# DeltaNet and FFN on one core: four 64x64 tiles for the recurrence, joins in halves, an earlier inverse, weights on another queue

## The chip, the cores and the metric

The kernel runs on one core of a Trainium2 chip. All data are fp32. The metric is the device time of one execution in microseconds (us). The core has five engines, each with its own instruction stream, which run beside each other and wait for one another by semaphores. The profile names them PE (TensorE matmuls; PEld is its weight loads), DVE (VectorE), ACT (ScalarE), POOL (GpSimd) and SP (SyncE, which here only issues DMAs). "SPq" is SP's queue of DMA issues. An engine runs its instructions strictly in the order in which they were placed, so an instruction that waits holds back all that stand behind it on its engine.

## The reference

Per batch and head (4 x 8, 768 tokens, head size 48), a state matrix is read and updated token by token. The attention output then goes through a layer norm and an FFN of 384 → 1536 → 384 with a residual:

```python
k_n = k / (np.linalg.norm(k, axis=-1, keepdims=True) + 1e-06)
for t in range(S):
    y[:, :, t] = q_t @ state
    v_old = k_t @ state
    state = state + beta_t * outer(k_t, v_t - v_old)
x = y.transpose(0, 2, 1, 3).reshape(4, 768, 384)
xn = (x - mean(x)) / sqrt(var(x) + 1e-06) * g_ln
out = x + relu(xn @ w_ch1) @ w_ch2          # 384x1536, 1536x384
```

(The three lines of the loop are the reference's einsum calls, written as products.) The two weight matrices arrive as 64-bit floats; the kernel reads them as pairs of 32-bit words.

## The kernel before, in words

**Chunks.** The 768 tokens are cut into 12 chunks of 64, and two chunks make a slab. Within a chunk the token loop becomes matrix work: U = X (V − K S) with X the inverse of a triangular 64x64 matrix, Y = Q S + P U (P is the masked product of Q and K), and the state grows by Kᵀ U. One instruction covers 8 heads and a pair of batches: the 128 partitions hold 64 tokens of one batch and 64 of another, and a "group" g is the half of the 16 head rows that are worked together.

**Stages of a slab.** `prep` transposes k and q on PE (`p_t`, L252), evicts them on ACT (`kqt`) and forms the products `p_g` (L263); the K Kᵀ half is evicted by ACT (`gsb`, L268) and stored to DRAM (`gd`, L308), the other half is masked by DVE (`pt`, L271). `blocks` loads the 32x32 diagonal blocks of K Kᵀ of the whole slab from DRAM (`gb`, L338), takes the norms from their diagonal on ACT (`nrm`, L344), and inverts all blocks on DVE in 31 steps of two operations (`tmp` L360, `xb` L365). The result goes to DRAM (`xd`, L369) and back into the layout of the recurrence (`xt`, L372). `join` computes the off-diagonal 32x32 block of the inverse: a DVE transpose (`xn`, L384), 32 matmuls of 32x32 (`p_e`, L391), an ACT eviction (`es`, L395), 32 more (`p_z`, L402), a DVE copy into `xt` (L405).

**Stages of a chunk.** `recur(c, g)` computes K S and Q S against the state (`p_b`, `p_y`, L424), V − K S on DVE (`rhs`, L429), U (`p_u` L438, ACT eviction `u` L440), the state's growth (`p_s` L450, DVE add `s` L457), adds P U to `p_y` (L466), evicts it on ACT (`x_ln`, L471), and prepares the layer norm (L475 to L490, `p_n` and `xnt`). `ffn(c)` has 12 groups of 3 matmuls (`p_h`, L502), each with a relu on ACT (`h_f`, L507), then 2 x 12 matmuls (`p_o`, L513), the residual on DVE (`o`, L520) and the output DMA.

**Weights.** The two matrices come in 24 pieces of 128x384. For each, a DMA brings the word pairs into one of two `words` buffers (`fetch_words`, L147, on SP's queue), and six DVE operations (`to_fp32`, L209, L214, L219, L224, L227, L231) build the fp32 piece `w_sb`. The FFN of the first chunks waits for them.

**What sets the order.** A `Plan` gives every step a due time and writes the program in the order of these times (L549 to L579); a scheduler then fixes each engine's stream from that. The times of a chunk are `T` = 50 apart. For a slab whose first chunk is due at t, the products are due from t−90 to t−55, the inverse from t−55 to t−18 and the join from t−10 to t. The part of the program ahead of the plan (L532 to L547) runs the products and the inverse of slab 0, mixed with the first weight pieces. PSUM has 8 banks: four buffers of tag "att", two banks of tag "two" (`p_g` and `p_s`), two of tag "ffn".

## Time and profile before

| | |
|---|---|
| three runs | 783.5, 784.26, 785.45 us (median 784.26) |
| the profiled execution | 784.72 us, of which the span from first to last instruction is 782.9 us |
| PE busy with matmuls | 622.4 us (79% of the span), 7080 records |
| DVE busy | 337.8 us (43%) |
| ACT busy | 167.5 us (21%) |
| POOL busy | 37.6 us (5%) |
| mean granted TensorE clock | 0.858 |

An fp32 matmul stands as two records in this profile, so the 32 matmuls of one `p_e` read "x64". A row of a timeline gives start, length, engine, line, operation, output and inputs, the tile of the array, the shape, the count, and in brackets the idle time ahead of it with what ended it. A row of stretches gives a stretch from A to B, its length, then the busy time (and the number of records) of each engine, the granted clock as a share of full speed, the share of DMA time and the rate in GB/s.

### The profile page before, as it was taken

What the parts mean: (1) busy time and instruction counts of PE and PEld (TensorE: products, weight loads), DVE (VectorE), ACT (ScalarE), POOL (GpSimd) and SP (SyncE); (2) the same over time, 40 slices, a digit from 0 to 9 for tenths busy, and PEclk for the clock granted to TensorE, in tenths of its full rate; (3) what the DMA queues carried; (4) which work ended last, traced back from release to release, by engine and by line L of the source; (5) the groups of instructions that cost most, each with busy time, mean ns of one, the idle gap of its engine ahead of it and who ended that gap; (6) DMA issues with size and microseconds to landing.
All of it is one profiled execution on the core that took longest, in us unless ns stands there. A gap on an engine that the chain in (4) does not pass through costs nothing.

```text
span 782.9 us, 16117 instructions
## 1 busy us (share of the span) xinstructions
PE 622.4 (79%) x7080; PEld 470.8 (60%) x7080; DVE 337.8 (43%) x822; ACT 167.5 (21%) x380; POOL 37.6 (5%) x56
## 2 busy tenths in 40 slices
PE   4300589969989907999956999965999975999997
PEld 3200577647678606867725877734877745868684
DVE  4597569678331862122772112681211671111100
ACT  4110133211143101422201323201222201212120
POOL 4111001000000110000010000000000000000000
PEclk8555559989899955999985999985999995999999
DMA  9891546441243321044121035122012011000000
GB/s 146 184 159 46 103 110 166 90 82 34 50 99 55 53 58 17 1 89 96 21 67 29 1 77 108 21 43 54 1 39 65 1 43 34 2 11 11 12 10 20
DMA packets 136822, 45.18 MB, mean 58 GB/s; under 512 B 128304, under 2 KB 131376, under 8 KB 136752
## 3 DMA queue, kind: packets, MB, share of 16 engines
q1 hardware_dynamic: 130448, 43.24, 26.9%
q10 hardware_dynamic: 6304, 0.92, 1.0%
q8 instruction: 55, 0.90, 0.5%
q14 instruction: 15, 0.12, 0.1%
HBM read 29.98 MB, written 14.16 MB: 56 GB/s over the span
## 4 chain that ended last, share of the span: by engine, by line
PE 61%; DVE 27%; DMA 6%; issue 3%; ACT 2%; SPq 1%; DVEq 0%; ACTq 0%
PE p_h L502 22%; PE p_o L513 16%; DVE tmp L360 7%; DVE xb L365 7%; DMA words<-in_moe_w_ch_dram 3%; PE p_z L402 3%; PE p_e L391 3%; PE p_g L263 3%; PE p_u L438 3%; PE p_y L466 3%; PE p_t L252 3%; PE p_b L424 2%; PE p_s L450 2%; PE p_y L424 1%; DMA xd<-xb 1%
## 5 line engine op out<-in xcount | busy, mean ns | idle before, releaser
L502 PE MATMUL p_h<-xnt,w_sb 128*128 128x256 f32 x864 | 211.4, 395 | 0.0
L513 PE MATMUL p_o<-w_sb,h_f 128*128 128x384 f32 x576 | 202.4, 496 | 7.1 <-DVE w_sb L231 7.1
L502 PEld LDWEIGHTS p_h<-xnt,w_sb 128*128 128x128 f32 x864 | 162.8, 195 | 26.2 <-ACT ksq L283 0.9
L513 PEld LDWEIGHTS p_o<-w_sb,h_f 128*128 128x128 f32 x576 | 105.3, 191 | 70.8 <-DVE w_sb L231 8.3
L391 PE MATMUL p_e<-xn,gsb 32*32 32x32 f32 x768 | 21.6, 229 | 123.6 <-DVE xn L384 123.6
L391 PEld LDWEIGHTS p_e<-xn,gsb 32*32 32x32 f32 x768 | 20.3, 144 | 127.3 <-issue 70.6
L507 ACT ACTIVATE h_f<-p_h 128x256 f32<-128x256 f32 x144 | 55.2, 383 | 168.7 <-PE p_h L502 168.7
L365 DVE TENSOR_TENSOR xb<-xb,tmp 128x31 f32<-128x31 f32 (+15 forms) x186 | 68.1, 366 | 5.4
L360 DVE TENSOR_TENSOR tmp<-xb,gb 128x31 f32<-128x31 f32 (+15 forms) x186 | 66.4, 357 | 5.5
L457 DVE TENSOR_TENSOR s<-s,p_s 48x384 f32<-48x384 f32 x44 | 24.2, 551 | 100.8 <-PE p_s L450 100.4
L395 ACT ACTIVATE es<-p_e 32x512 f32<-32x512 f32 x24 | 14.1, 589 | 128.5 <-PE p_e L391 128.2
L271 DVE TENSOR_TENSOR pt<-p_g,pmask 128x512 f32<-128x512 f32 x24 | 16.6, 692 | 56.4 <-ACT gsb L268 46.3
L405 DVE COPY xt<-p_z 32x512 f32<-32x512 f32 x24 | 16.4, 684 | 56.0 <-PE p_z L402 55.8
L520 DVE TENSOR_TENSOR o<-p_o,x_ln 128x384 f32<-128x384 f32 x24 | 13.3, 555 | 56.3 <-PE p_o L513 56.2
L475 DVE BATCH_NORM_STATS2 st<-x_ln 128x6 f32<-128x384 f32 x24 | 13.4, 559 | 55.0 <-ACT x_ln L471 54.9
L253 ACT COPY kqt<-p_t 128x512 f32<-128x512 f32 x48 | 28.0, 585 | 38.0 <-PE p_t L252 36.8
L263 PE MATMUL p_g<-kqt 48*64 48x128 f32 (+1 forms) x896 | 30.1, 275 | 6.4 <-ACT gsb L268 3.6
L263 PEld LDWEIGHTS p_g<-kqt 48*64 48x64 f32 x896 | 23.8, 146 | 15.9 <-issue 6.6
L466 PEld LDWEIGHTS p_y<-u,pt 64*64 64x64 f32 x768 | 26.0, 142 | 7.1 <-issue 6.9
L402 PE MATMUL p_z<-xt,es 32*32 32x32 f32 x768 | 25.8, 233 | 5.3 <-ACT es L395 4.5
L466 PE MATMUL p_y<-u,pt 64*64 64x48 f32 x768 | 29.1, 227 | 0.0
L402 PEld LDWEIGHTS p_z<-xt,es 32*32 32x32 f32 x768 | 22.6, 147 | 10.1 <-ACT es L395 7.8
(65 smaller groups left out, 503.3 us busy)
## 6 DMA issues: line engine op xcount, KB each, us to landing
words<-in_moe_w_ch_dram SPq DMA_DIRECT2D x24, 384.0 KB, 3.9
gd<-gsb SPq DMA_DIRECT2D x12, 512.0 KB, 3.2
qpad<-in_q_dram SPq DMA_DIRECT2D x24, 192.0 KB, 4.4
v_raw<-in_v_dram SPq DMA_DIRECT2D x24, 192.0 KB, 4.6
out_dram<-o SPq DMA_DIRECT2D x48, 96.0 KB, 2.2
kpad<-in_k_dram SPq DMA_DIRECT2D x22, 192.0 KB, 4.2
xd<-xb SPq DMA_DIRECT2D x6, 512.0 KB, 2.6
gb<-gd SPq DMA_DIRECT2D x44, 64.0 KB, 3.4
```

The lines of the kernel that those rows point to most:

```text
L252: nc.tensor.transpose(p_t[:, j], src[:, h : h + 2], ident)
L253: nc.scalar.copy(made[c][0][g][:, :, n], p_t)
L263: nc.tensor.matmul(p_g[toks, hp, j, n0:n1], kqt[rows, j, 0, toks], kqt[rows, j, n0:n1, toks])
L360: nc.vector.tensor_tensor(out=t, in0=xb[:, 0:n, j : j + 1].to_broadcast([128, n, w]), in1=gb[:, j : j + 1, j + 1 : BK].to_broadcast([128, ...
L365: nc.vector.tensor_tensor(out=rest, in0=rest, in1=t, op=ALU.subtract)
L391: nc.tensor.matmul(p_e[r1, h], gsb[r0, h, BK:C], xn[r0, h])
L402: nc.tensor.matmul(p_z[r0, h], es[r1, h], xt[r1, h, BK:C])
L457: nc.vector.tensor_tensor(out=new, in0=new, in1=p_s[rows, :, 0 : NP * D].rearrange("p e (j d) -> p e j d", d=D), op=ALU.add,)
L466: nc.tensor.matmul(p_y[toks, h], pt[toks, h], u[toks, h], start=(c == 0 and h == 0), stop=True, skip_group_check=True,)
L502: nc.tensor.matmul(p_h, w1_sb[:, t, f * 128 : (f + 1) * 128], xnt[:, t], start=(t == 0), stop=(t == KC - 1),)
L507: nc.scalar.activation(h_f, p_h, ACTF.Relu)
L513: nc.tensor.matmul(p_o, hs[f][:, g * 128 : (g + 1) * 128], w2_sb[:, f], start=(f == 0), stop=(f == FT - 1),)
```

## The change

1. **K S and Q S on four tiles.** Before, the state was zero-padded to 128 rows so that two heads went through one 128x64 tile: 16 matmuls of N = 96 per chunk and group. Now the state is kept without padding, and 32 matmuls of 48 rows and N = 48 are spread over the four 64x64 tiles in the order (0,0), (1,1), (0,1), (1,0) (`TILES`). Both results share a two-bank PSUM tile `p_by` of a new tag "by" with one buffer. U and P U keep their 16 matmuls each, but go through all four tiles in that order, and so does `p_s`.
2. **Halves put back.** With four tiles the odd heads' halves (the two batches) come out exchanged. `unswap` puts them back when U and Y are evicted: an ACT copy of 128x192, a DVE copy of 64x192 and an ACT copy of 64x192 replace one ACT copy of 128x384.
3. **Joins in halves.** `join` takes a slab's two chunks, and each chunk in two halves of 8 heads. The `p_z` matmuls of one half stand between the `p_e` matmuls of the next, and the evictions are of half the size.
4. **Plan.** `T` is 45. Products are due from t−88 to t−62, the inverse from t−62 to t−26 and the join from t−8 to t. Slab 1 and the first chunks have new times, and the loads of the next slab come later or earlier by new rules.
5. **First loads.** The weight words are fetched from POOL's queue and not SP's. The first q and v loads stand behind the first loads of the inverse, and five weight pieces, not four, stand ahead of it in the program.

PSUM is now two banks "att", two "two" (which `p_u` shares), two "by", two "ffn".

The order of the engines' streams shows what the plan's numbers do. The first place is ACT in the steady part of the program, around the square root `nrm` that opens the inverse of a slab (the fourth of five such in the plan). `h_f` is the relu of one of an FFN's 12 groups, and `xnt` the layer norm's last step ahead of that FFN. Before:

```order
L268 COPY gsb<-p_g 128x2x4x64
L490 COPY xnt<-p_n 128x3x128
L283 ACTIVATE ksq<-kpad_77 128x384 x2
L507 ACTIVATE h_f<-p_h 128x256
L286 ACTIVATE knrm<-ksum 128x16
L507 ACTIVATE h_f<-p_h 128x256 x2
L440 COPY u<-p_u 128x384
L507 ACTIVATE h_f<-p_h 128x256 x4
L471 COPY x_ln<-p_y 128x384
L479 ACTIVATE rstd<-mv,eps 128x1
L507 ACTIVATE h_f<-p_h 128x256 x2
L344 ACTIVATE nrm<-gb 128x32
```

And with the change:

```order
L265 COPY gsb<-p_g 128x2x4x64
L430 COPY u<-p_u 128x4x48
L432 COPY u<-p_u 64x4x48
L430 COPY x_ln<-p_by 128x4x48
L432 COPY x_ln<-p_by 64x4x48
L503 ACTIVATE rstd<-mv,eps 128x1
L514 COPY xnt<-p_n 128x3x128
L531 ACTIVATE h_f<-p_h 128x256 x2
L341 ACTIVATE nrm<-gb 128x32
```

Nine relus stood between the last eviction of the products (`gsb`) and `nrm`; now there are two, with the evictions of U and Y of a group ahead of them.

The second place is PE at the join of a slab. `p_o` is the second half of the FFN that stands ahead of it. Before:

```order
L466 MATMUL p_y<-u,pt 64x48 x16
L513 MATMUL p_o<-w_sb,h_f 128x384 x10
L391 MATMUL p_e<-xn,gsb 32x32 x32
L402 MATMUL p_z<-xt_133,es 32x32 x32
L391 MATMUL p_e<-xn,gsb 32x32 x32
L489 MATMUL p_n<-ident,xn_ln 128x128 x3
L402 MATMUL p_z<-xt_134,es 32x32
L424 MATMUL p_b<-s_141,kqt 64x96 x5
L402 MATMUL p_z<-xt_134,es 32x32 x31
L502 MATMUL p_h<-xnt,w_sb 128x256 x3
```

And with the change:

```order
L537 MATMUL p_o<-w_sb,h_f 128x384 x10
L448 MATMUL p_by<-s_131,kqt 64x48 x32
L392 MATMUL p_e<-xn,gsb 32x32 x32
L412 MATMUL p_z<-xt_123,es 32x32 x16
L464 MATMUL p_u<-rhs,xt_123 64x48 x16
L490 MATMUL p_by<-u,pt 64x48 x16
L392 MATMUL p_e<-xn,gsb 32x32 x2
L412 MATMUL p_z<-xt_123,es 32x32 x2
```

The next chunk's `p_by` now stands ahead of the join, and U and P U of its first group stand between the join's halves.

The third place is DVE at the start, where the inverse of slab 0 begins (`tmp`, `xb`) and the weight pieces are decoded (`part`, `power`, `man`, `full`, `w_sb`). Before, six pieces stood ahead of `gb<-gb,db`, which opens the inverse, and two were woven into it:

```order
L352 TENSOR_TENSOR gb<-gb,db 128x1024
L209 TENSOR_SCALAR part<-words 128x384
L360 TENSOR_TENSOR tmp<-xb,gb 128x31
L214 TENSOR_SCALAR power<-part 128x384
L365 TENSOR_TENSOR xb<-xb,tmp 128x31
L219 TENSOR_SCALAR man<-words 128x384
L360 TENSOR_TENSOR tmp<-xb,gb 128x60
L224 SCALAR_TENSOR_TENSOR full<-words,man 128x384
```

With the change nine stand ahead of it, ten are woven into it in the same manner (one operation of a piece, one of the inverse), and three more follow before the first `xn`:

```order
L349 TENSOR_TENSOR gb<-gb,db 128x1024
L216 TENSOR_SCALAR man<-words 128x384
L357 TENSOR_TENSOR tmp<-xb,gb 128x31
L268 TENSOR_TENSOR pt<-p_g,pmask 128x2x4x64
L362 TENSOR_TENSOR xb<-xb,tmp 128x31
L221 SCALAR_TENSOR_TENSOR full<-words,man 128x384
L357 TENSOR_TENSOR tmp<-xb,gb 128x60
L224 SCALAR_TENSOR_TENSOR full<-words,full 128x384
```

So 22 of the 24 pieces stand ahead of the first `xn` on DVE, where there were 10.

The diff, cut to what matters:

```diff
     def ps_att(shape, name):
-        return psum.tile(shape, FP32, name=name, tag="att", bufs=4)
+        return psum.tile(shape, FP32, name=name, tag="att", bufs=2)
 
     def ps_two(shape, name):
         return psum.tile(shape, FP32, name=name, tag="two", bufs=1)
+
+    def ps_by(shape, name):
+        return psum.tile(shape, FP32, name=name, tag="by", bufs=1)
 
...
             words.append(early_pool.tile([128, WN, 2], U32, name="words", bufs=2))
-            nc.sync.dma_start(
+            nc.gpsimd.dma_start(
                 out=words[-1].rearrange("p n w -> p (n w)"), in_=pieces[len(words) - 1][1]
...
-    for c in range(2):
-        load(qpads[c], q, c, (nc.sync,))
-    for c in range(2):
-        vs[c] = loads.tile([128, GH, D], FP32, name="v_raw")
-        load(vs[c], v, c, (nc.sync,))
...
-    states = [const.tile([128, 2, NP, 2, D], FP32, name=f"s{g}") for g in range(2)]
+    states = [const.tile([128, 2, NP, D], FP32, name=f"s{g}") for g in range(2)]
...
+    N_JOIN = 2
+    def join(chunks):
+        last = None
+        for c in chunks:
+            xt, gsb = xts[c % NXT], grams.pop(c)[0]
+            xn = work.tile([128, GH, BK], FP32, name="xn", bufs=1)
+            nc.vector.transpose(xn, xt[:, :, 0:BK])
+            for g in range(2):
+                heads = range(g * H, (g + 1) * H)
+                p_e = ps_att([128, H, BK], "p_e")
+                for h in heads:
+                    for e in range(2):
+                        r0 = slice(e * C, e * C + BK)
+                        r1 = slice(e * C + BK, (e + 1) * C)
+                        nc.tensor.matmul(p_e[r1, h % H], gsb[r0, h, BK:C], xn[r0, h])
+                    if last:
+                        last_z(*last, h % H)
+                if last:
+                    end_z(*last)
+                es = work.tile([128, H, BK], FP32, name="es", bufs=2)
+                for e in range(2):
+                    r1 = slice(e * C + BK, (e + 1) * C)
+                    nc.scalar.mul(es[r1], p_e[r1], -1.0)
+                last = (xt, g, es, ps_att([128, H, BK], "p_z"))
+                yield
+        for h in range(H):
+            last_z(*last, h)
+        end_z(*last)
+        yield
+    def last_z(xt, g, es, p_z, h):
         for e in range(2):
             r0 = slice(e * C, e * C + BK)
+            r1 = slice(e * C + BK, (e + 1) * C)
+            nc.tensor.matmul(p_z[r0, h], es[r1, h], xt[r1, g * H + h, BK:C])
+    def end_z(xt, g, es, p_z):
+        for e in range(2):
+            r0 = slice(e * C, e * C + BK)
+            nc.vector.tensor_copy(out=xt[r0, g * H : (g + 1) * H, BK:C], in_=p_z[r0])
...
+    TILES = ((0, 0), (1, 1), (0, 1), (1, 0))
+    def half(e):
+        return slice(C * e, C * e + C)
+    def unswap(dst, src):
+        nc.scalar.copy(dst[:, :, 0], src[:, 0])
+        nc.vector.tensor_copy(out=dst[half(0), :, 1], in_=src[half(1), 1])
+        nc.scalar.copy(dst[half(1), :, 1], src[half(0), 1])
 
...
+        p_by = ps_by([128, 2, 512], "p_by")[:, :, 0 : 2 * NP * D].rearrange(
+            "p n (m j d) -> p n m j d", m=2, d=D
+        )
         if c:
-            p_b = ps_att([128, H, D], "p_b")
-            for n, dst in ((0, p_b), (1, p_y)):
+            for n in range(2):
                 for j in range(NP):
-                    for e in range(2):
-                        toks = slice(C * e, C * e + C)
+                    for hp, e in TILES:
+                        rows = slice(DP * hp, DP * hp + D)
                         nc.tensor.matmul(
-                            dst[toks, 2 * j : 2 * j + 2], kqt[:, j, n, toks], s[:, e, j],
-                            start=(j == 0), stop=(n == 0), skip_group_check=True,
+                            p_by[half(e ^ (hp & n)), hp, n, j], kqt[rows, j, n, half(e)], s[rows, e, j],
+                            start=(n == 0 and j == 0), stop=(n == 0), skip_group_check=True,
                         )
...
+        p_u = ps_two([128, 2, 512], "p_u")[:, :, 0 : NP * D].rearrange("p n (j d) -> p n j d", d=D)
+        for j in range(NP):
+            for hp, e in TILES:
+                nc.tensor.matmul(
+                    p_u[half(e ^ hp), hp, j], xt[half(e), 2 * j + hp], rhs[half(e), 2 * j + hp]
+                )
         u = work.tile([128, H, D], FP32, name="u")
+        unswap(u.rearrange("p (j n) d -> p j n d", n=2), p_u)
         yield
         if c < NCH - 1:
             p_s = ps_two([128, 2, 512], "p_s")
+            for j in range(NP):
+                for hp, e in TILES:
+                    nc.tensor.matmul(
+                        p_s[DP * hp : DP * hp + D, e, j * D : (j + 1) * D],
+                        kp[half(e), 2 * j + hp, 0:D], u[half(e), 2 * j + hp],
+                    )
             for hp in range(2):
+                new = s[DP * hp : DP * hp + D]
                 nc.vector.tensor_tensor(
                     out=new, in0=new,
+                    in1=p_s[DP * hp : DP * hp + D, :, 0 : NP * D].rearrange("p e (j d) -> p e j d", d=D),
+                    op=ALU.add,
                 )
             yield
+        for j in range(NP):
+            for hp, e in TILES:
                 nc.tensor.matmul(
+                    p_by[half(e ^ hp), hp, 1, j], pt[half(e), 2 * j + hp], u[half(e), 2 * j + hp],
+                    start=(c == 0 and j == 0), stop=True, skip_group_check=True,
                 )
         y = xs[c][:, g]
+        unswap(y.rearrange("p (j n d) -> p j n d", n=2, d=D), p_by[:, :, 1])
         yield
...
-        first.spread(prep_g(c), 4, 0, 4)
-    first.spread(weights(0, 4), 4, 2, 6)
+        first.spread(prep_g(c), 4, 4 * c, 4 * c + 4)
+    first.spread(weights(0, 5), 5, 0, 8)
     first.run()
-    for _ in blocks(0, (nc.sync, nc.scalar)):
+    inverse = blocks(0, (nc.sync, nc.scalar))
+    next(inverse)
+    for c in range(2):
+        load(qpads[c], q, c, (nc.sync,))
+    for c in range(2):
+        vs[c] = loads.tile([128, GH, D], FP32, name="v_raw")
+        load(vs[c], v, c, (nc.sync,))
+    for _ in inverse:
         pass
     first = Plan()
     for c in range(2):
         first.spread(prep_p(c), 5, 0.1 * c, 4)
-    first.spread(weights(4, 6), 2, 2, 4)
+    first.spread(weights(5, 6), 1, 3, 4)
     first.run()
     for c in (2, 3):
         load_all(c)
-    for _ in join(0):
-        pass
-
-    T = 50
-    starts = [0, 16, 90] + [120 + T * i for i in range(NCH - 2)]
-    ends = [12, 36, 120] + starts[4:]
+
+    T = 45
+    starts = [0, 16, 84] + [114 + T * i for i in range(NCH - 2)]
+    ends = [12, 36, 114] + starts[4:]
     plan = Plan()
-    plan.spread(join(1), N_JOIN, 2, 8)
+    plan.spread(join(range(2)), 5, -1, 0)
     plan.spread(weights(6, NW // 2), NW // 2 - 6, 0, 20)
     plan.spread(weights(NW // 2, NW), NW - NW // 2, 20, 52)
     for c in range(NCH):
         t0, t1 = starts[c], ends[c]
         plan.once(t0, begin, c)
-        if c < 2:
-            for g in range(2):
-                plan.spread(recur(c, g), N_RECUR, t0 + g, t1)
-        else:
-            plan.spread(in_turn(recur(c, 0), recur(c, 1)), 2 * N_RECUR, t0, t1)
+        plan.spread(in_turn(recur(c, 0), recur(c, 1)), 2 * N_RECUR, t0, t1)
     ffn_0 = ffn(0)
     plan.spread(ffn_0, FT, 12, 32, whole=False)
-    plan.spread(ffn_0, FT, 48, 66)
-    plan.spread(ffn(1), N_FFN, 66, 120)
+    plan.spread(ffn_0, FT, 48, 64)
+    plan.spread(ffn(1), N_FFN, 64, 114)
     for c in range(2, NCH):
         plan.spread(ffn(c), N_FFN, starts[c + 1], starts[c + 1] + T)
     for m in range(1, NSL):
         chunks = range(SLAB * m, SLAB * m + SLAB)
         t = starts[SLAB * m]
-        times = (t - 90, t - 55, t - 18, t - 10) if m > 1 else (12, 33, 74, 82)
+        times = (t - 88, t - 62, t - 26, t - 8) if m > 1 else (4, 22, 62, 76)
         if m > 1:
             for c in chunks:
-                plan.once(t - 99, load_all, c)
+                plan.once(t - 89 - 40 * (c % SLAB == 0 and m > 2), load_all, c)
         plan.spread(in_turn(*(prep(c) for c in chunks)), SLAB * N_PREP, times[0], times[1])
         plan.spread(blocks(m, (nc.sync,)), N_BLOCKS + 1, times[1], times[2])
-        plan.spread(in_turn(*(join(c) for c in chunks)), SLAB * N_JOIN, times[3], t)
+        plan.spread(join(chunks), 5, times[3], t)
     plan.run()
```

54 lines of the change are left out of this document (4 added, 50 removed).

## The prediction

> **What bounds the kernel now.** I read the chain that ended last first, then the waits, then the span cut at the starts of the joins.
>
> ```profile
> PE 61%; DVE 27%; DMA 6%; issue 3%; ACT 2%; SPq 1%; DVEq 0%; ACTq 0%
> ```
>
> ```profile
> PE p_e L391 <- DVE xn L384: 123.6, 10, 56.5
> ```
>
> The chain runs over PE, but 27% of it is DVE, and PE's longest waits stand at one place: the join waits for `xn`, the end of the inverse. I cut the span there (stretch, length, then busy us and records of PE, PEld, DVE, ACT, POOL, clock, DMA share, GB/s):
>
> ```profile
> 0.00:84.87 84.87, 15.10 (x288) 12.52 (x289) 58.43 (x146) 14.17 (x27) 17.28 (x31) 0.61 0.78 139
> 84.87:201.10 116.23, 103.57 (x1114) 79.95 (x1114) 80.68 (x195) 27.66 (x64) 5.23 (x6) 0.85 0.41 91
> 201.10:294.77 93.67, 69.89 (x1061) 53.60 (x1060) 46.44 (x112) 22.11 (x49) 5.06 (x6) 0.87 0.32 62
> 294.77:414.90 120.13, 103.43 (x1180) 77.63 (x1181) 46.32 (x113) 27.51 (x63) 4.82 (x6) 0.88 0.24 50
> 414.90:534.45 119.55, 103.11 (x1181) 77.31 (x1182) 46.31 (x113) 27.51 (x63) 4.81 (x6) 0.89 0.24 50
> 534.45:651.03 116.58, 103.07 (x1180) 77.27 (x1181) 42.90 (x109) 25.31 (x57) 0.36 (x1) 0.90 0.13 31
> 651.03:782.90 131.87, 124.18 (x1079) 92.50 (x1079) 16.76 (x35) 23.24 (x57) 0.00 (x0) 0.94 0.05 11
> ```
>
> A steady slab takes 120 us, of which PE is busy 103. For the slab from 414.90, the same view of PE and of DVE alone (the last two rows are the inverse's lines L360 and L365):
>
> ```profile
> 428.25:496.82 68.57, 68.57 (x719) 0.98 0.25 53
> 496.82:521.31 24.49, 24.48 (x196) 1.00 0.23 42
> 521.31:534.45 13.14, 0.00 (x1) 0.58 0.36 85
> ```
>
> ```profile
> 496.82:527.60 30.78, 28.27 (x78) 0.93 0.21 40
> 496.82:527.60 30.78, 10.51 (x31) 0.93 0.21 40
> 496.82:527.60 30.78, 11.75 (x31) 0.93 0.21 40
> ```
>
> And the events of the inverse, from the timelines of ACT, SP, DVE and PE, with the median from issue to landing of the load `gb`:
>
> ```profile
> 475.40 0.59 ACT L268 COPY gsb<-p_g 128x512 f32<-128x512 f32 x1 [1.77 <-PE p_g L263]
> ```
>
> ```profile
> 478.96 1.89 SPq L338 DMA_DIRECT2D gb<-gd  x4
> 527.60 0.34 SPq L369 DMA_DIRECT2D xd<-xb  x1
> ```
>
> ```profile
> gb<-gd SPq DMA_DIRECT2D x44, 64.0 KB, 3.4
> ```
>
> ```profile
> 253.88 0.25 ACT L344 ACTIVATE nrm<-gb 128x32 f32<-128x32 f32 x1
> ...
> 496.82 0.25 ACT L344 ACTIVATE nrm<-gb 128x32 f32<-128x32 f32 x1
> ```
>
> The products are done at 476.0, and the block load lands at about 480.85 + 3.4 = 484.2. But `nrm` runs at 496.8, since it stands on ACT behind nine relus, which come as fast as PE's `p_h`: 12.6 us late by order alone. From there it is 30.8 us to the store of the inverse (527.60) and 6.85 us through DRAM and the transpose to the first `p_e` (534.45). PE runs out of work at 521.3 and stands 13.1 us. So a slab is 81.9 (join to `nrm`) + 30.8 + 6.85 = 119.55 us, and whoever moves `nrm` forward shortens it, until PE's own work (about 106) is the limit.
>
> **The change part by part.** The PE rows used:
>
> ```profile
> 201.11 1.20 PE L391 MATMUL p_e<-xn,gsb 32*32 32x32 f32 x64
> ...
> 414.90 1.92 PE L391 MATMUL p_e<-xn,gsb 32*32 32x32 f32 x64 [13.41 <-DVE xn L384]
> ...
> 428.25 2.93 PE L502 MATMUL p_h<-xnt,w_sb 128*128 128x256 f32 x6
> ...
> 435.13 1.13 PE L438 MATMUL p_u<-rhs,xt 64*64 64x48 f32 x32
> 436.19 2.86 PE L502 MATMUL p_h<-xnt,w_sb 128*128 128x256 f32 x12
> 438.98 0.79 PE L450 MATMUL p_s<-u,kpad 64*48 64x48 f32 x32
> ...
> 455.86 0.88 PE L424 MATMUL p_b<-s,kqt 128*64 128x96 f32 x16
> ...
> 457.33 2.85 PE L513 MATMUL p_o<-w_sb,h_f 128*128 128x384 f32 x8
> ...
> 492.58 1.14 PE L466 MATMUL p_y<-u,pt 64*64 64x48 f32 x32
> 493.64 5.45 PE L502 MATMUL p_h<-xnt,w_sb 128*128 128x256 f32 x24
> ```
>
> *Tiles.* K S with Q S take 455.86 to 457.33 = 1.47 us per group; U takes 435.13 to 436.19 = 1.06, and P U 492.58 to 493.64 = 1.06. The growth takes 0.79. That is 4.4. The records of U and P U, over two diagonal tiles, cost 33 ns each; those of the growth, which already alternates over more tiles, 24.7; those of the 32x32 `p_e` at full clock 1.20/64 = 18.8. The price of 64x48 records over four tiles is not in the trace. Its bounds are 18.8 ns (overlap as in `p_e`) and 33 (none). I take 18.8 to 20, since the rows fall with the number of tiles: 64 x 19 = 1.2 for K S and Q S, 0.6 each for the other three, 3.0 in all. Gain 1.3 us per group, 5 per slab; at 24.7 it is 0.4, and at 33 about −0.9.
>
> The Trainium skill, "TensorEngine Tiling (Array Packing)", section Instruction Overhead, speaks against this part: about 60 cycles go to each matmul, and one should not take tiles out of a dimension that is already small. With its figure of 60 cycles, I estimate 25 ns a record at 2.4 GHz and 1.6 us for K S and Q S, no gain there. The 18.8 ns of `p_e` don't agree with it.
>
> *Halves put back.* Each eviction of U and Y becomes three smaller ones over ACT and DVE. For their price I take the `nrm` row (0.25, nearly no data) as the floor and `gsb` (0.59, more data) as the ceiling. Off the chain of the slab they cost nothing: ACT is busy 27.5 of 120 us. On DVE, 8 of some 0.3 us per slab are 2.4 us, about half inside the inverse. The wait of the growth and of P U for U grows by a few tenths; PE has FFN matmuls between. Without that cover it would be 24 x 0.5 = 12 us. Two PSUM waits are new: `p_by` has one buffer, so a group's K S waits for the eviction of the last group's Y, and `p_u` shares two banks with `p_s` and `p_g`, so it waits for their evictions (0.6 as `gsb`). In the new order FFN matmuls of 1.4 us or more stand between, which hides them; inside the join they don't, and what waits behind them there is the rest of the join. They are among its 1.5 us of waits below.
>
> *Join.* 414.90 to 428.25 = 13.35 us now, at a clock that has fallen (`p_e` 1.92 against 1.20) and with waits for each eviction in turn. In halves, with U and P U of one group and most of a `p_by` between, I reckon 256 records at 19 to 30 ns (4.9 to 7.7), 2.2 of other work and about 1.5 of waits: about 10, bounds 9 and 13.
>
> *Plan.* In the new order of the streams, between the join and `nrm` PE has the same work as in 428.25:496.82, less seven groups of `p_h` (two relus for nine). One group is (438.98 − 436.19)/2 = 1.4, so 9.8. U, growth and P U of the second chunk's group also stand behind it now (2.9), what moved into the join is gone (2.6), and the tiles save 3: 68.57 − 18.3 = 50. So `nrm` comes 10 + 50 = 60 us after the join's start. The load will not hold it: the last `gsb` stands some 18 us of PE work ahead, and its way to the landed load was 8.2. The inverse: 22.3 busy us in its two lines, and 3.4 for the operations that open it, with 6.8 of other DVE work woven in now that PE is not idle beside it: 32.5. Then 6.85. Sum 99.4. PE's limit: 10 for the join, and 93.06 (68.57 + 24.49) less 5.2 for tiles and 2.2 moved, 85.7, and 1.5 where `rhs` and `xn` stand between `p_by` and `p_e`: 97.2. The later of the two decides: 99.5 for the slabs of 120, 98.5 for that of 116.6, which has less DVE work. Nothing else is late next: PE's wait of 13 goes to about 2. The slab from 201.10 has its `nrm` at 253.88, 52.8 after the join; the new order has seven relus ahead of it for twelve (−7), and −2.7 of tiles and join: 84.
>
> *First loads.* On DVE the start looks thus:
>
> ```profile
> 43.08 1.23 DVE L352 TENSOR_TENSOR gb<-gb,db 128x1024 f32<-128x1024 f32 x1 [0.60 <-DVE db L349]
> 44.22 0.35 DVE L209 TENSOR_SCALAR part<-words 128x384 uint32<-128x384 uint32 x1
> ...
> 47.35 0.35 DVE L209 TENSOR_SCALAR part<-words 128x384 uint32<-128x384 uint32 x1
> ...
> 74.28 0.21 DVE L365 TENSOR_TENSOR xb<-xb,tmp 128x31 f32<-128x31 f32 x1
> ```
>
> ```profile
> words<-in_moe_w_ch_dram SPq DMA_DIRECT2D x24, 384.0 KB, 3.9
> ```
>
> A woven piece costs about 1.8 us (47.35 − 44.22, less 1.3 of inverse in between). Ten instead of two make the inverse of slab 0 some 14 longer, with fewer other operations in it: its end moves from 74.5 to 86, and the first join, 10 us behind it, to 97. This needs words to land in time. The trace has no fetch on POOL's queue. If one takes L to land, two buffers give a piece every (L + 2.8)/2 us, with 2.8 the six operations. L = 3.9, as on SP, costs nothing; 6 gives 93 for the end of the inverse, 8 gives 106. POOL's fetches wait for a buffer, and behind them on POOL stand the scaling of v and the diagonal copy for the inverse; both come later than the fetch needs its buffer. I take 97, bounds 95 and 115. In return the weights are there when the FFN starts (DVE is free of 12 pieces in that slab), so the second stretch keeps PE's 103.6 less 4 for tiles and 4 for join and clock: 95.5.
>
> The Trainium skill, "SBUF — State Buffer", section "SBUF: two separate sides", warns of this very queue: descriptors of a DMA issued from GpSimd are written by GpSimd's cores, which are locked out while DVE runs some operations, so the DMA waits for DVE. No run here shows such a fetch yet.
>
> *The tail* has no inverse: 131.9 − 5 (tiles) − 3.4 (join) − 1 (clock) = 122.5.
>
> **Sum.** 97 + 95.5 + 84 + 99.5 + 99.5 + 98.5 + 122.5 = 696.5, and 1.8 around the span (784.72 − 782.9): 698 us, where the profiled execution has 784.72 and the median of the runs is 784.26.
>
> **The rivals.**
> - *Records don't overlap* (0.15). At 25 to 33 ns a record the tiles give nothing, PE's limit per slab is 105 and decides: five slabs 5.5 longer and the tail 5, 730. For it: 33 ns for U now. Against it: 18.8 for `p_e`.
> - *Words come late* (0.14). L of 6 to 8 us puts the first join at 104 to 116; the rest is as forecast: 705 to 717, say 716.
> - *The change doesn't move the inverse* (0.06). `nrm` still waits, for a load that is late on SP behind v, k and q. Then only tiles (5 per slab) and joins (3) remain, cut to some 20 in all by the chain that still ends in DVE: 765. Against it: the load has 10 us to spare.
> - *Slower* (0.05). POOL's fetches starve DVE: 22 of 24 pieces stand ahead of the first `xn` in DVE's stream, so DVE, and with it the inverse, goes at the rate of the fetches. The gain of 86 is lost when the first join comes at 183, that is with 22 pieces in some 173 us, 7.9 each, L = 13 us. From there on the kernel is slower: at L = 15, 807.
>
> **How the numbers follow.** The forecast has 0.60. The range of 678 to 732 takes in the second rival and the first to its end; below, it has L at 3.9 with slabs at PE's bound and a join of 9. Left out are the third and fourth and some of the rest. Runs lie within 0.3% of each other, which is what a measurement can tell from no change: faster by more 0.93, the same 0.02, slower 0.05.
>
> **What would show it.** `nrm` some 60 us after a steady join's start, not 82; PE's wait for `xn` at the joins near 2 us, not 13; `p_by` of 64 records in about 1.2 us; U and P U in 0.6. The first `p_e` near 97, and DVE's waits for `words` near nothing. It is wrong if steady slabs stay above 106, if records of 64x48 keep 25 ns or more, or if the first join comes after 115.

## The result

The change makes the kernel faster: 722.55 us (median of four runs, 720.92 to 724.42) against 784.35 before, a ratio of 0.921 with an interval of 0.9185 to 0.924. The profiled execution has a span of 719.1 us. The forecast was 698, and 678 to 732 its range: the direction and most of the size were right, and 24 us of the expected gain are missing.

The span of the changed kernel, cut at the starts of its joins as before (stretch, length, busy us and records of PE, PEld, DVE, ACT, POOL, clock, DMA share, GB/s):

```profile
0.00:107.97 107.97, 17.02 (x289) 13.73 (x289) 86.94 (x219) 14.27 (x27) 37.92 (x55) 1.00 0.79 153
107.97:201.87 93.90, 89.58 (x1254) 69.41 (x1255) 54.41 (x134) 30.43 (x77) 4.73 (x6) 1.00 0.28 62
201.87:290.28 88.41, 70.84 (x1176) 50.10 (x1176) 49.52 (x125) 23.38 (x60) 5.83 (x6) 0.91 0.32 67
290.28:394.33 104.05, 98.87 (x1309) 72.63 (x1309) 49.18 (x125) 29.52 (x75) 5.04 (x6) 0.91 0.29 56
394.33:497.03 102.70, 97.02 (x1309) 71.04 (x1309) 49.23 (x125) 29.50 (x75) 5.04 (x7) 0.93 0.28 57
497.03:596.08 99.05, 95.86 (x1245) 70.01 (x1245) 45.71 (x119) 27.21 (x69) 1.31 (x2) 0.93 0.15 36
596.08:719.10 123.02, 116.77 (x1208) 86.31 (x1207) 20.69 (x48) 25.11 (x69) 0.00 (x0) 0.95 0.06 14
```

| stretch | before | forecast | measured | missed by |
|---|---|---|---|---|
| to the first join | 84.9 | 97 | 108.0 | +11.0 |
| first join to second | 116.2 | 95.5 | 93.9 | −1.6 |
| second to third | 93.7 | 84 | 88.4 | +4.4 |
| third to fourth | 120.1 | 99.5 | 104.05 | +4.6 |
| fourth to fifth | 119.6 | 99.5 | 102.7 | +3.2 |
| fifth to sixth | 116.6 | 98.5 | 99.05 | +0.6 |
| tail | 131.9 | 122.5 | 123.0 | +0.5 |

So the miss lies in two places: the start (11 of 22.6) and the three stretches from the second join to the fifth (12.2 together).

The clock column of the first two stretches can't be relied on. It reads 1.00 there, though `p_e` of the first join takes 1.92 us, as it does at 290.28, where the column reads 0.50, and not 1.20 as at 394.33:

```profile
107.97 1.92 PE L392 MATMUL p_e<-xn,gsb 32*32 32x32 f32 x64 [56.29 <-DVE xn L384]
```

**A steady slab.** The events of the slab from 394.33, as the timelines of ACT, SP and PE have them:

```profile
437.40 0.58 ACT L265 COPY gsb<-p_g 128x512 f32<-128x512 f32 x1 [1.77 <-PE p_g L260]
...
457.33 0.25 ACT L341 ACTIVATE nrm<-gb 128x32 f32<-128x32 f32 x1
```

```profile
440.99 1.89 SPq L335 DMA_DIRECT2D gb<-gd  x4
```

```profile
489.29 0.53 SPq L366 DMA_DIRECT2D xd<-xb  x1
```

```profile
394.33 1.20 PE L392 MATMUL p_e<-xn,gsb 32*32 32x32 f32 x64 [1.94 <-DVE xn L384]
...
397.09 1.55 PE L464 MATMUL p_u<-rhs,xt 64*64 64x48 f32 x32 [0.52 <-DVE xt L417]
...
404.98 0.90 PE L513 MATMUL p_n<-ident,xn_ln 128*128 128x128 f32 x3
...
407.60 5.75 PE L526 MATMUL p_h<-xnt,w_sb 128*128 128x256 f32 x18
...
439.40 0.68 PE L464 MATMUL p_u<-rhs,xt 64*64 64x48 f32 x32
...
442.14 0.57 PE L475 MATMUL p_s<-u,kpad 64*48 64x48 f32 x32
...
445.43 0.68 PE L490 MATMUL p_by<-u,pt 64*64 64x48 f32 x32
...
454.31 1.15 PE L448 MATMUL p_by<-s,kqt 48*64 48x48 f32 x64
...
497.03 1.20 PE L392 MATMUL p_e<-xn,gsb 32*32 32x32 f32 x64 [2.26 <-DVE xn L384]
```

`nrm` now stands 63.0 us behind the join (82 before), the inverse takes 32.0, the way through DRAM to `p_e` 7.7; PE waits 2.3 at the join, not 13. What came forward is the products: the last `gsb` starts 43.1 us behind the join, where it was 60.5. `nrm` is still late by the order on ACT, for `gb` is issued by 442.9 and lands 2.7 to 3.3 us after its issue, some 11 us ahead of `nrm` (12.6 before). The seven relus that no longer stand ahead of `nrm` are PE work that now comes later, but other PE work stands between `gsb` and `nrm` in their place. The records of the recurrence are as fast as hoped: 1.15/64 = 18 ns for K S and Q S, 0.68 us for U and for P U. But the join is longer than forecast. From the first `p_e` to the first `p_h` it takes 13.3 us, and U at 397.09 needs 1.55 us where U at 439.40 needs 0.68. The clock goes with it (same columns as above):

```profile
392.39:394.33 1.94, 0.00 (x2) 0.01 (x1) 1.88 (x4) 0.43 (x2) 0.66 (x2) 1.00 0.78 122
394.33:397.09 2.76, 1.89 (x96) 1.67 (x96) 0.44 (x2) 1.50 (x4) 1.07 (x1) 1.00 0.42 92
397.09:400.83 3.74, 2.92 (x64) 2.35 (x65) 1.38 (x3) 0.63 (x2) 0.00 (x0) 0.52 0.02 4
400.83:403.58 2.75, 2.59 (x117) 2.37 (x117) 1.82 (x5) 1.38 (x4) 0.00 (x0) 0.50 0.00 0
403.58:407.60 4.02, 4.02 (x107) 3.38 (x103) 1.59 (x5) 1.52 (x4) 0.00 (x0) 0.50 0.02 6
407.60:410.00 2.40, 2.40 (x10) 1.95 (x7) 0.83 (x2) 0.00 (x0) 0.00 (x0) 0.50 0.02 7
```

From 397.1 to 410 the granted clock is 0.50. PE waits 1.9 us ahead of the join and some 0.9 between its first steps, and after that it runs at half speed for 13 us, though it is busy most of the time. At the join at 596.08, where PE does not wait for `xn`, the clock falls too (0.51 from 602 to 604), after gaps of 0.7, 0.5 and 0.4 us.

**The start.** DVE's and ACT's rows around the first inverse:

```profile
36.08 0.26 ACT L341 ACTIVATE nrm<-gb 128x32 f32<-128x32 f32 x1 [3.54 <-DMA gb<-gd]
```

```profile
37.38 0.36 DVE L206 TENSOR_SCALAR part<-words 128x384 uint32<-128x384 uint32 x1 [1.15 <-DMA words<-in_moe_w_ch_dram]
...
41.56 0.36 DVE L206 TENSOR_SCALAR part<-words 128x384 uint32<-128x384 uint32 x1 [1.16 <-DMA words<-in_moe_w_ch_dram]
...
48.03 0.17 DVE L342 TENSOR_SCALAR nrm<-nrm 128x32 f32<-128x32 f32 x1
...
50.32 2.34 DVE L349 TENSOR_TENSOR gb<-gb,db 128x1024 f32<-128x1024 f32 x1
...
96.56 0.20 DVE L362 TENSOR_TENSOR xb<-xb,tmp 128x31 f32<-128x31 f32 x1
...
107.20 0.70 DVE L384 STREAM_TRANSPOSE xn<-xt 128x512 f32<-128x512 f32 x1
```

```profile
35.87 0.54 POOL L150 DMA_DIRECT2D words<-in_moe_w_ch_dram  x1 [4.57 <-DVE full L224]
```

`nrm` is ready at 36.3, and DVE takes it up at 48.0: the weight pieces stand ahead of it in DVE's order, and they wait for their words. A piece comes every 4.2 us (37.38, 41.56). The words fetched at 35.87 are used at 41.56 as soon as they land, so landing takes some 5.7 us here, while 3.9 is the median of all 24 fetches. The inverse opens at 50.3 (43.1 before) and ends at 96.8, not 86. The first `xn` stands behind three more pieces, which cost it little: its load `xt` is issued from 99.9 to 101.9 and lands up to 5.0 us later.

### The profile page after: what moved, and what is told of

It is laid out like the page before. It is cut to its first block, busy times and chain, and to the rows that moved or that the text cites. A ratio compares the mean times of both kernels' runs of the same rounds, so it can differ in the third digit from the quotient of the medians.

```text
span 719.1 us, 17676 instructions
## 1 busy us (share of the span) xinstructions
PE 586.0 (81%) x7784; PEld 433.2 (60%) x7784; DVE 355.7 (49%) x894; ACT 179.4 (25%) x452; POOL 59.9 (8%) x80
## 4 chain that ended last, share of the span: by engine, by line
PE 54%; DVE 30%; DMA 7%; issue 3%; ACT 3%; SPq 2%; POOL 0%; DVEq 0%; ACTq 0%; POOLq 0%
PE p_h L526 19%; PE p_o L537 17%; DVE tmp L357 9%; DVE xb L362 8%; PE p_t L249 3%; PE p_g L260 3%; PE p_by L448 2%; DMA words<-in_moe_w_ch_dram 2%; PE p_z L412 2%; PE p_u L464 2%; PE p_e L392 2%; PE p_by L490 2%; SPq L116 1%; PE p_n L513 1%; PE p_s L475 1%
## 5 line engine op out<-in xcount | busy, mean ns | idle before, releaser
L362 DVE TENSOR_TENSOR xb<-xb,tmp 128x31 f32<-128x31 f32 (+15 forms) x186 | 64.2, 345 | 4.5
L392 PEld LDWEIGHTS p_e<-xn,gsb 32*32 32x32 f32 x768 | 18.5, 132 | 76.6 <-DVE xn L384 73.0
L448 PEld LDWEIGHTS p_by<-s,kqt 48*64 48x64 f32 x1408 | 26.7, 143 | 13.1 <-issue 9.8
L453 DVE TENSOR_TENSOR rhs<-v_raw,p_by 128x384 f32<-128x384 f32 x22 | 12.1, 552 | 43.7 <-PE p_by L448 40.8
L400 ACT ACTIVATE es<-p_e 32x256 f32<-32x256 f32 x48 | 18.0, 375 | 61.4 <-PE p_e L392 55.7
L448 PE MATMUL p_by<-s,kqt 48*64 48x48 f32 x1408 | 31.5, 231 | 2.0 <-ACT x_ln L432 2.0
L250 ACT COPY kqt<-p_t 128x512 f32<-128x512 f32 x48 | 27.9, 585 | 19.2 <-PE p_t L249 12.6
L417 DVE COPY xt<-p_z 32x256 f32<-32x256 f32 x48 | 20.0, 417 | 25.3 <-PE p_z L412 24.8
L280 ACT ACTIVATE ksq<-kpad 128x384 f32<-128x384 f32 x24 | 12.5, 521 | 67.9 <-DVE ksum L281 51.1
L351 POOL COPY xb<-db 128x32 f32<-128x32 f32 x6 | 3.5, 584 | 273.9 <-DVE db L346 273.9
```

Source lines behind the costliest of these rows:

```text
L250: nc.scalar.copy(made[c][0][g][:, :, n], p_t)
L362: nc.vector.tensor_tensor(out=rest, in0=rest, in1=t, op=ALU.subtract)
L392: nc.tensor.matmul(p_e[r1, h % H], gsb[r0, h, BK:C], xn[r0, h])
L417: nc.vector.tensor_copy(out=xt[r0, g * H : (g + 1) * H, BK:C], in_=p_z[r0])
L448: nc.tensor.matmul(p_by[half(e ^ (hp & n)), hp, n, j], kqt[rows, j, n, half(e)], s[rows, e, j], start=(n == 0 and j == 0), stop=(n == 0), ...
```

## The experiments

The scheduler writes all streams anew for each kernel, so an edit of one part also moves a few instructions elsewhere. Each kernel was timed in three rounds beside the kernel before.

**Words on SP's queue again.**

```diff
-            nc.gpsimd.dma_start(
+            nc.sync.dma_start(
                 out=words[-1].rearrange("p n w -> p (n w)"), in_=pieces[len(words) - 1][1]
```

> The changed kernel with the weight words fetched from SP's queue again, all else as changed. In its order seven weight pieces stand ahead of the inverse of slab 0 and one is woven into it (the changed kernel: nine and ten), and 15 stand behind the first xn (2). Theory A (the late first join of 108.0 us comes from the pieces that DVE decodes ahead of and inside the inverse, not from the chip's start): first p_e at 76 to 82 us, and the weights come later, so the stretch to the second join grows from 93.9 to 105 or more; sum of both 183 to 195 against 201.9; whole kernel 705 to 716. Rival B (the start is bound by something else, such as the products or the block load): first p_e stays above 100, kernel within 3 us of 722. Rival C (late weights hold the FFN): second join after 202, kernel 723 to 740.

Measured: 712.38 us (707.87 to 714.7). The first stretches of this kernel, and the first wait of the FFN for weights in its PE timeline:

```profile
0.00:75.23 75.23, 16.54 (x288) 13.25 (x288) 54.20 (x132) 13.10 (x24) 14.46 (x29) 0.79 0.78 128
75.23:195.73 120.50, 95.87 (x1225) 68.41 (x1225) 84.78 (x220) 30.28 (x77) 7.42 (x8) 0.76 0.46 107
```

```profile
147.74 2.93 PE L537 MATMUL p_o<-w_sb,h_f 128*128 128x384 f32 x4 [7.32 <-DVE w_sb L228]
```

The first join comes at 75.2, 33 us earlier, and the second at 195.7 against 201.9. Of the 33 us, 27 are given back, since DVE decodes the pieces later (busy 84.8 in the second stretch, against 54.4) and the FFN waits for them. Both joins lie just outside what Theory A expected, the first 0.8 us early and the second 0.7 late; the kernel's time is inside, and outside the ranges of both rivals. Fetching the words on POOL's queue costs 10 us. Six of them show in these two stretches, and there it is DVE's order that does it: nine pieces ahead of the inverse and ten in it, for seven and one.

**The recurrence as before** (wide matmuls against the padded state, one eviction), in the changed plan:

```diff
-    states = [const.tile([128, 2, NP, D], FP32, name=f"s{g}") for g in range(2)]
+    states = [const.tile([128, 2, NP, 2, D], FP32, name=f"s{g}") for g in range(2)]
...
+                            dst[toks, 2 * j : 2 * j + 2], kqt[:, j, n, toks], s[:, e, j],
...
-        unswap(u.rearrange("p (j n) d -> p j n d", n=2), p_u)
+        nc.scalar.copy(u, p_u)
...
-        return psum.tile(shape, FP32, name=name, tag="att", bufs=2)
+        return psum.tile(shape, FP32, name=name, tag="att", bufs=4)
...
-            pt = work.tile([128, H, C], FP32, name="pt", bufs=7)
+            pt = work.tile([128, H, C], FP32, name="pt", bufs=6)
```

> The changed kernel (plan, halved joins, first loads) with the recurrence as before: K S and Q S of 128 rows and N = 96 against the zero-padded state, U and P U over two tiles, one ACT copy per eviction, four att buffers, and six pt buffers for seven (for space). Theory A (tiles save 4.3 - 2.8 = 1.5 us of PE per group and chunk, and PE's order carries nrm and so the slab): 22 groups x 1.5 = 33 slower at most, 745 to 758 us. Rival (the tiles lie off the path, since the slab ends with the inverse, and the three-part evictions cost as much as they save): 715 to 732.

Measured: 732.86 us (731.83 to 734.32), 10 more than the changed kernel. Its fourth and seventh stretch:

```profile
397.20:499.55 102.35, 100.24 (x1181) 74.58 (x1181) 46.88 (x117) 28.19 (x67) 4.86 (x6) 0.97 0.29 56
...
600.81:730.00 129.19, 123.00 (x1084) 90.45 (x1083) 17.83 (x40) 23.84 (x61) 0.00 (x0) 0.97 0.06 14
```

The steady slab is as long with the old tiles (102.35) as with the new (102.70). Of the other two steady slabs one is 0.7 us shorter and one 2.2 longer. Most of the 10 us come from the tail (129.2 against 123.0) and the stretch after the first join (99.1 against 93.9). In the steady slabs PE is busy 100.2 us for 97.0: the new tiles free 1.5 us per group, but a part of that comes back as PE time at the lower clock (0.93 for 0.97), and the rest as idle time. Neither theory's interval was hit exactly; the rival's reason holds for the steady slabs, Theory A's for the two ends.

**The plan's numbers of before**, with tiles, halved joins and first loads as changed:

```diff
-    T = 45
-    starts = [0, 16, 84] + [114 + T * i for i in range(NCH - 2)]
+    T = 50
+    starts = [0, 16, 90] + [120 + T * i for i in range(NCH - 2)]
...
-        times = (t - 88, t - 62, t - 26, t - 8) if m > 1 else (4, 22, 62, 76)
+        times = (t - 90, t - 55, t - 18, t - 10) if m > 1 else (12, 33, 74, 82)
...
-                plan.once(t - 89 - 40 * (c % SLAB == 0 and m > 2), load_all, c)
+                plan.once(t - 99, load_all, c)
```

> The changed kernel with the plan's numbers of before (T = 50, products t-90 to t-55, inverse t-55 to t-18, join t-10 to t, loads at t-99, slab 1's old times); tiles, halved joins and first loads as changed. Theory A (the plan moved nrm from 82 to 63 us behind a join): nrm at 74 to 80 and steady slabs of 112 to 117 us for 103; kernel 755 to 775. Rival (the gain came from tiles and joins alone): steady slabs at 103 to 106, kernel 720 to 735.

**The plan's numbers of the change alone**, in the kernel before (the same lines the other way round):

> The kernel before with the plan's numbers of the change alone (T = 45, products t-88 to t-62, inverse t-62 to t-26, join t-8 to t, slab 1's and the loads' new times); tiles, joins, first loads as before. Theory A (the plan is what moved the steady slabs from 120 to 103, and the tiles lie off the path there): steady slabs 101 to 106, first join at 85, kernel 715 to 735. Rival (without the shorter tiles PE's work is the bound again, or the whole joins cost more in this place): steady slabs 107 to 112, kernel 740 to 760.

Measured: 782.22 us (777.15 to 786.54) without the new plan, 726.9 us (724.61 to 729.07) with it alone. One steady slab of each, the old plan first:

```profile
432.86:546.51 113.65, 97.12 (x1309) 72.37 (x1309) 49.48 (x125) 29.49 (x75) 4.80 (x6) 0.88 0.25 53
```

```profile
383.05:488.49 105.44, 102.07 (x1182) 76.27 (x1181) 46.43 (x113) 27.47 (x63) 4.66 (x6) 0.95 0.28 55
```

The plan alone brings 57 of the change's 62 us (784.35 to 726.9 and to 722.55). Beside it the other parts nearly cancel: the tiles with their evictions are worth 10, the words on POOL's queue cost 10. Without it tiles, halves and first loads together bring next to nothing: they shorten the steady slab from 119.6 to 113.65, and the start, 25 us later at the first join than in the kernel before (110.2 for 84.9), eats it. Two of its three steady slabs are as expected, the third 1.2 us shorter; the kernel was slower than expected because the second and third stretch grew as well, to 110.0 and 98.7 from the 93.9 and 88.4 of the changed kernel.

**Whole joins**, that is the function `join` of the kernel before, in the changed kernel:

```diff
-    N_JOIN = 2
+    N_JOIN = 3
...
-    def join(chunks):
+    def join(c):
```

> The changed kernel with the join of before (a chunk's 32 p_e, one eviction es, 32 p_z, one copy), tiles, plan and first loads as changed. Theory A (a join's length is set by its chain of waits and by the clock, granted at 0.50 in it): halves save a little, 1 to 3 us per join, kernel 728 to 740. Rival (halves bring nothing, since the half clock sets the length): 719 to 726. Rival 2 (the finer halves cost more than they hide): below 719.

Measured: 723.6 us (722.01 to 727.71), not to be told from 722.55. The halves bring nothing that can be measured.

**One copy per eviction**:

```diff
-        nc.scalar.copy(dst[:, :, 0], src[:, 0])
-        nc.vector.tensor_copy(out=dst[half(0), :, 1], in_=src[half(1), 1])
-        nc.scalar.copy(dst[half(1), :, 1], src[half(0), 1])
+        nc.scalar.copy(dst.rearrange("p j n d -> p n j d"), src)
```

> The changed kernel with one ACT copy of 128x384 per eviction of U and Y, as before; the odd heads' halves stay exchanged, so the numbers belong to the wrong batch and this part of the work is left out. Theory A (the three-part eviction costs a few tenths in the join alone): 716 to 722 us. Rival (it eats what the tiles save, by DVE time inside the inverse and by the wait for U): 705 to 713.

Measured: 718.08 us (717.18 to 720.63), a ratio to the kernel before of 0.9145 (0.911 to 0.918) against 0.921. Putting the halves back costs some 4 us. They don't lie in the steady slabs (105.1, 104.3 and 99.4). The second and third stretch are shorter (91.9 and 83.5 us for 93.9 and 88.4), but the kernel with whole joins, which puts the halves back too, also has 84.0 in the third, so where the cost lies is not shown.

**Joins filled with FFN work**:

```diff
-        plan.spread(ffn(c), N_FFN, starts[c + 1], starts[c + 1] + T)
+        plan.spread(ffn(c), N_FFN, starts[c + 1] + 12, starts[c + 1] + T + 12)
```

> The changed kernel with the FFN of chunks 2 to 11 due 12 later in the plan, so that 10 of its p_o stand between the p_e, p_z, p_u and P U of a join. Theory A (the join is long since PE idles ahead of it and at its waits, after which the clock is granted at 0.50 for some 13 us; about 6 us of a steady slab): clock near 1.00 over the join, steady slabs 95 to 99 us for 103, kernel 695 to 710. Rival (the slab is held by nrm, inverse and the way through DRAM, 63 + 32 + 7.7, and work moved into the join only shifts nrm): steady slabs 101 to 105, kernel 716 to 726.

Measured: 702.24 us (698.26 to 705.21). One steady slab, and the clock in its join:

```profile
388.81:483.51 94.70, 92.49 (x1304) 66.77 (x1303) 49.63 (x125) 29.12 (x75) 4.83 (x6) 0.98 0.30 62
...
388.81:401.00 12.19, 11.73 (x336) 8.19 (x335) 4.19 (x10) 4.33 (x12) 0.00 (x0) 1.00 0.09 20
401.00:408.00 7.00, 7.00 (x64) 5.90 (x60) 3.12 (x8) 3.69 (x8) 0.00 (x0) 0.76 0.01 4
```

With `p_o` between the steps of the join the clock stays at 1.00 for 12 us, and the slab takes 94.7 us instead of 102.7. Of the 8 us, 4.5 are PE's busy time (97.0 to 92.5, the same work) and 3.5 its idle time. The filling hides the waits and keeps the clock up; which of the two does how much of the idle part was not told apart. Two things limit this reading. The edit also moves `nrm`, to 49.7 us behind the join from 63.0, so a part of the idle time may have gone by the order. And from 401 to 404 the clock is 0.50 all the same, though PE was idle for only 0.5 of the 12.2 us before; whether the waits bring it down or the short matmuls themselves is open.

**Old tiles with joins filled**: the edit of the second experiment and that of the last one together.

> The kernel with the recurrence as before (old tiles, 16 wide matmuls for K S and Q S, one ACT copy per eviction, six pt buffers) in the changed plan, with the FFN of chunks 2 to 11 due 12 later, so that the joins are filled with p_o: against the run with new tiles and filled joins (702.2) it shows what the tiles are worth once PE no longer idles at the joins. Theory A (with joins filled PE's own work bounds the steady slabs, so each slab pays the tiles' 5 to 6 us): steady slabs 98 to 102 us for 91 to 98, kernel 722 to 735. Rival (the tiles stay off the path, as in the run with old tiles and unfilled joins, where the slabs were equal): steady slabs 91 to 98, difference in slab 0 and tail alone, kernel 710 to 716.

Measured: 715.42 us (713.89 to 720.29), 13 more than with the new tiles. The same slab:

```profile
392.46:489.32 96.86, 96.66 (x1182) 72.01 (x1181) 46.82 (x117) 28.30 (x67) 4.82 (x6) 1.00 0.30 61
```

Here PE is the bound (busy 96.7 of 96.9 us). The new tiles take 4.2 us of PE's work away and the slab gains 2.2. The other 2 come back as idle time of PE, in the run with new tiles and filled joins, none of it at `xn`: 1.3 at relus, the rest at `u` and `es`. The longest of these waits:

```profile
457.48 1.56 PE L526 MATMUL p_h<-xnt,w_sb 128*128 128x256 f32 x6 [1.10 <-ACT h_f L531]
```

The time is the rival's: even with filled joins the tiles bring most of their gain at the two ends.

**Four more, toward a faster kernel.** The first has the words on SP with three buffers (and one buffer less for the FFN's output) and filled joins. The second has four pieces for one ahead of the plan, and the loads of chunks 2 and 3 behind them. The third and the fourth are these two with products, inverse and the loads for them due 8 earlier:

```diff
-            words.append(early_pool.tile([128, WN, 2], U32, name="words", bufs=2))
+            words.append(early_pool.tile([128, WN, 2], U32, name="words", bufs=3))
...
-    first.spread(weights(5, 6), 1, 3, 4)
+    first.spread(weights(5, 9), 4, 3, 4)
...
-        times = (t - 88, t - 62, t - 26, t - 8) if m > 1 else (4, 22, 62, 76)
+        times = (t - 96, t - 70, t - 34, t - 8) if m > 1 else (4, 22, 62, 76)
```

> The changed kernel with the words on SP's queue and three word buffers for two (one buffer less for the FFN's output o), and the FFN of chunks 2 to 11 due 12 later. Theory A (first join at 75 as with the words on SP; with three buffers the words wait less behind the first joins; joins filled): first join 75 to 79, second at 180 to 192, steady slabs 95 to 99, kernel 675 to 698. Rival (joins not bound by the clock, words still late): first two joins at 75 and 196, steady slabs 102 to 105, kernel 705 to 715.

> The run with words on SP, three buffers and filled joins (689.8), with four weight pieces for one in the plan ahead of the joins and the loads of chunks 2 and 3 behind them: four pieces, not one, are woven into the inverse of slab 0, so that fewer are woven into that of slab 1. Theory A (DVE's weight decoding is what stretches the second stretch, 118.7 us with DVE busy 82.6 and an inverse of 43 for 30): first join 79 to 82, second join 184 to 191 for 194.8, kernel 678 to 686. Rival (moving the pieces only shifts the time from the second stretch to the first): second join 193 to 197, kernel 688 to 693.

> The run with words on SP, three buffers and filled joins (689.8), with products and inverse of slabs 2 to 5 due 8 earlier in the plan (t-96, t-70, t-34). Theory A (with the joins filled the steady slab is again held by nrm, 48 to 52 us behind a join, the inverse of 36 and the 9 through DRAM, while PE is busy 91 to 95 of 93 to 99): the slab from 194.8, where PE idles 8 of 84 us, falls to 76 to 81, steady slabs to 90 to 96, kernel 675 to 684. Rival (PE's own work is the bound now, and an earlier inverse only waits): 687 to 693.

> The run with the words early as well (689.0), with the same shift of 8. Theory A: the slab from 189.8 falls from 87.7 to 80 to 84, steady slabs to 90 to 96, kernel 673 to 684. Rival: 686 to 692.

Measured: 689.83, 688.99, 682.76 and 681.4 us (the last from 679.27 to 683.55, a ratio of 0.868 with 0.865 to 0.871). The first has its joins at 76.1 and 194.8, so the third buffer did not help the start, and steady slabs of 98.7, 93.1 and 90.6. Fetching the words early moved the second join to 189.8, as its Theory A had it, but the next three stretches grew by 6 together and the time came out as its rival's; why they grew is open. Products and inverse earlier gave 7 to 8 us each time; in the last kernel the slab that took 87.7 takes 79.4:

```profile
190.73:270.10 79.37, 67.95 (x1168) 46.97 (x1167) 50.26 (x125) 21.94 (x58) 5.82 (x6) 0.99 0.31 65
```

The steady slabs there are 91 to 95 us with PE busy 86 to 92, so both limits are near. This kernel is 5.7% faster than the change (681.4 against 722.55).

## Why the prediction was right, and where it was not

**What bounds the kernel** was right. The wait for `xn` at the joins was the cost, and a plan that brings `nrm` forward shortens the slab: with its numbers and nothing else, the steady slab fell from 119.6 to 105.4. But `nrm` did not come forward by losing its wait on ACT, which is 11 us still, for 12.6; the work ahead of it became less.

**Plan.** `nrm` 60 us after the join was forecast, 60.2 to 64.3 measured in the three steady slabs; 32.5 and 6.85 for the inverse and the way back, 32.0 and 7.7 measured. The 50 us between join and `nrm` were right (407.60 to 457.33 = 49.7).

**Join** is the first step that failed: "about 10, bounds 9 and 13", and 13.3 measured. The prediction knew the low clock from `p_e` (1.92 against 1.20) and let 30 ns a record stand for it at the upper end, but took the middle for its sum and left the rest of the join at full speed. With 1.9 us of idle time left ahead of the join the clock falls all the same, and with it U, P U, K S and `p_n` inside the join, and the first `p_h` behind it (407.60 to 413.19 for 18 records, 5.6 us, where six take 1.4 later and 18 would take 4.2). The waits inside were right: 1.8 us for 1.5. The run with filled joins shows what the clock, the waits and the shift of `nrm` are worth together: 20 us. The Trainium skill, "TensorE: Matmul & The Clock Gate", section "Part 1: The HAM clock gate", lets the clock fall after a whole idle window of about 3.4 us. Here it falls after one gap of 1.94 us and shorter ones, so on this point the trace goes further than the page.

**First loads** is the second: 97 forecast for the first join, 108.0 measured, 11 of the 22.6 missed. All of them lie ahead of the end of the inverse (96.8 for 86). The formula of a piece every (L + 2.8)/2 held ahead of the inverse (L = 5.7 gives 4.2, as measured), but L was taken from the median row, 3.9; in the kernel before, too, the fetches of the first 30 us took 4.6 to 6.8. The formula's values for L of 6 and 8 lie 13 us apart, so it counts 13 pieces, the ten in the inverse and the three more ahead of it; at 5.7 it would have put the end of the inverse near 91. Of the 11 us, 7.2 are `gb<-gb,db` at 50.3 for 43.1 before. Another 3.5 had no term: three DVE operations that run beside a product on POOL take longer (2.34 us for 1.23, and twice 1.8 for 0.6). The rival of late words had the first mechanism, and its price of 716 is nearer to the result than the forecast's.

**The third stretch** (88.4 for 84) goes with the clock too: it is 0.91 there. The run with words on SP has 1.00 and 83.6 us in that stretch, the one with filled joins (which fills later joins, not this one's) 0.89 and 88.9. Most of the 4.4 us lies ahead of `nrm`, which comes 47.2 us behind the join for a forecast of 43.1, at a clock of 0.93; in the kernel with whole joins the clock there is 1.00 and `nrm` comes after 42.3. No run was made for it alone, so the cause is argued, not shown. PE still waits 11.9 us for `xn` at the end of this stretch (20.6 before).

**Tiles.** The price of a record was right: 4.3 to 2.8 us per group, 1.5 for the forecast's 1.3. The estimate of 25 ns a record that spoke against it does not hold here, with 18 measured. But what it is worth was over-read: 3 us per slab were credited on the way to `nrm` and 5 to PE's limit, and the runs with the old tiles show −0.7, −0.3 and 2.2 in the steady slabs with unfilled joins and 0.4 to 2.2 with filled ones, 5 in the stretch after the first join and 6 in the tail. PE's time saved ahead of a wait is idle time.

**Halves put back** was costed at nothing off the chain and at some 1.2 us of DVE in each inverse. It costs 4.5 us in all, and the steady slabs, where that cost was looked for, are not shorter without it. **Join in halves** had its own gain folded into the 10 us of the join; none is measurable.

**The rivals.** Records without overlap: no. An inverse that is not moved: no. Slower: no; the words' L never came near 13.

## What to carry to other kernels

When a chain of dependent stages bounds a slab, the order in which engines take up their work (here the products and the square root, ahead of FFN work and not behind it) is worth more than faster matmuls: 57 of 62 us. Before crediting a shorter operation, look at what waits behind it: time saved ahead of a wait turns into idle time. A row of short matmuls with small waits between them can cost the clock as well; long, independent matmuls kept back to stand between them helped here. And for a transfer that paces a chain, take the landing time from the stretch in question, not from the median of all.

## What the runs showed of the hardware

Two things were not expected. The first is the clock that falls to 0.50 for 13 us after a gap of 1.9 us and a few of half a microsecond, and at another join after the small gaps alone. The second is what weaving does to POOL. Its product `v_raw` takes 1.48 to 1.73 us in the kernel before, and up to 5.09 us in the changed one, where DVE runs weight operations and the inverse without a gap beside it. In the run with the words on SP, with one piece woven there, it takes 1.5 to 1.6 in that stretch. A DVE operation that meets it grows as well:

```profile
74.35 5.09 POOL L285 TENSOR_TENSOR v_raw<-v_raw,knrm 128x768 f32<-128x768 f32 x1
```

```profile
78.03 1.82 DVE L228 SCALAR_TENSOR_TENSOR w_sb<-full,scale_w,power 128x384 f32<-128x384 f32 x1
```

The fetches on POOL's queue themselves did not suffer: 0.54 us to issue and 3.9 us to land in the median, as on SP (3.9 before, 3.8 with the words back on SP). The page "SBUF — State Buffer" of the Trainium skill, section "SBUF: two separate sides", warns that such fetches starve beside some DVE operations. No row here shows it. Landing goes with how busy the DMAs are, on either queue: from 30 to 42 us the kernel before has a DMA share of 0.61 (a column that can pass 1) and fetches that land in 3.5 to 3.9 us; the changed kernel has 1.20 and 5.1 to 6.6, and the one with the words on SP 1.43 and 7.0.
